# W2's weight tiles requested one by one, six tiles ahead of TensorE

## The chip, the core and the metric

The kernel runs on one core of one Trainium2 chip. The metric is the device time of one execution in microseconds; where several executions are shown, their median is given. All operands are bf16 in HBM and all sums are f32 in PSUM.

## The reference

The program computes `x + A(LN(x)) + B(LN(x))` for a sequence of 2048 rows of width D = 576. A is a causal attention with 32 heads of 18 columns and a sliding window of 256 positions. B is a gated feed-forward block with F = 4608 hidden columns. The part that matters here is B's last product, whose weight is W2.

```python
xn = _layernorm(x)                                  # 2048 x 576
# A: sliding-window attention, 32 heads of 18 columns, window 256
o  = softmax(mask(q @ k.T * 18**-0.5)) @ v          # q, k, v = xn @ wqkv
A  = o @ wo                                         # wo: 576 x 576
# B: gated feed-forward
h  = silu(xn @ w1) * (xn @ w3)                      # 2048 x 4608
B  = h @ w2                                         # w2: 4608 x 576
out = x + A + B
```

## The kernel before, in words

The sequence is cut into NC = 4 blocks of 512 rows, and each block c goes through two phases (for every block but the first, a projection to q, k and v stands ahead of them).

**Phase 1** makes the hidden tiles. For u = 0 to 35, TensorE multiplies one 128-column slice of w1 and w3 with the normalised rows (`unit_pairs`, line 670), ScalarE takes a tanh (line 679), and VectorE forms a tile of `hT` (lines 685 and 688). Attention scores, exponentials, masks and three of four P·V groups are worked in between.

**Phase 2** sums the block's output. `p2_list` writes its order out by hand: two halves of 288 output columns, and in each half nine W2 tiles and then the four `wo` steps of the attention output. A W2 tile is 512 rows by 288 columns (288 KB, loaded by one DMA in `load_w2`, line 347). TensorE spends 32 matmuls on it (line 736: four 128-row slices, four row tiles of the output, each in two halves of 64 rows). So a block uses 18 W2 tiles, numbered 0 to 17. After a tile's 32 matmuls the list has an item `next`, at which the program asks for a later tile. The items that carry matmuls are counted by `n`, which starts at -3 and is raised by one behind each of them: two items of `wo` come first, then 16 for each W2 tile. After `n == 19` the last P·V group is put in (line 611), and its result is turned, scaled and sent to `oT` by the SP queue (line 658). Behind `n == 40` the SP queue sends a transposed piece of the next block's rows (line 392), from `n == 170` on it loads six parts of the next block's w1 and w3 (line 315), and at `n == 300` it swaps halves of the rows (line 399). Outputs are added by VectorE (line 755) and written by the SP queue (line 757).

**Buffers and order.** Eight slots hold W2 tiles: four of their own (`w2`) and four (`w2x`) laid over the second w1/w3 buffer, which is free once phase 1 has ended. `w2_at` gives tile i the slot i modulo 8. The tiles 0 to 3 are asked for during the block before (for block 0, in phase 1 on the SP queue). The tiles 4 to 17 are asked for in phase 2 on ScalarE's DMA queue, which works in program order:

- tiles 4 and 5 at the start of phase 2, behind the last matmul of phase 1 (an explicit wait, `after=(last_pe(),)`);
- tile `sl + 6` at the `next` item of tile `sl`, for `sl` = 0 to 11. No wait is written there; the only wait comes from the slot, which must have been read: tile i waits for the last matmul of tile i - 8. The tiles 6 and 7 have no such predecessor in their block.
- at the items of tiles 13, 14, 16 and 17, the next block's tiles 0 to 3, which wait for the slots of this block's tiles 10, 11, 16 and 17.

`_Prog.add` collects the dependencies of each operation, and `resolve` turns them into semaphore waits: an operation waits for the last one of each engine that it depends on, and each engine executes in program order. `last_pe()` is the operation that was added last for TensorE.

```python
                if sl + AHEAD < 2 * NFC:
                    load_w2(c, sl + AHEAD)
                elif sl in (13, 14, 16, 17):
                    load_w2(c + 1, sl - 13 if sl < 16 else sl - 14)
```

Of the kernel before, what the change touches and what calls it, by code (L numbers as in the profile page):

```python
# [44 lines left out]
class _Prog:  # L45
# [13 lines left out]
    def add(self, eng, fn, r=(), w=(), j=(), dma=None, after=()):  # L59
        deps = []  # L60
        for k in r:
            deps += self.bufs[k].writers
        for k in w:
            g = self.bufs.get(k)
            if g is not None:
                deps += g.ahead(eng)
        for k in j:
            g = self.bufs[k].before
            if g is not None:
                deps += g.ahead(eng)  # L70
        op = _Op(eng, fn, deps + list(after), dma)
        op.after = tuple(after)
        self.n[eng] += 1
        op.pos = self.n[eng]
        if dma is not None:
            self.dma_count[dma] = self.dma_count.get(dma, 0) + 16
            op.cnt = self.dma_count[dma]
        for k in r:
            self.bufs[k].readers.append(op)
        for k in w:  # L80
            self.bufs[k] = _Gen([op], self.bufs.get(k))
        for k in j:
            self.bufs[k].writers.append(op)
        for k in w:
            if self.bufs[k].before is not None:
                self.bufs[k].before.before = None
        self.ops.append(op)
        return op
# [76 lines left out]
def bass_parallel_sum__sliding_block__glu_gated_swiglu__prompt_kernel(  # L165
# [32 lines left out]
    with ExitStack() as es:  # L198
# [4 lines left out]
        NXP, NOF, NPT, NW13, NW2, NOD, AHEAD = 7, 4, 10, 3, 4, 2, 6  # L203
# [120 lines left out]
        def last_pe():  # L324
            return next(o for o in reversed(P.ops) if o.eng == "pe")
# [9 lines left out]
        def w2_at(c, i):  # L335
            n = i % (2 * NW2)
            if n < NW2:
                s = (n + 2 * c) % NW2
                return s, w2[s]
            return n, w2x[:, n - NW2, :, :]  # L340

        def load_w2(c, i, eng="act", after=()):
            if c >= NC:
                return
            s, dst = w2_at(c, i)
            half, fc = divmod(i, NFC)
            add(eng, lambda e: e.dma_start(
                dst[:, :, :], B_w2[fc * 512:(fc + 1) * 512, half * HD:(half + 1) * HD].rearrange("(fl p) d -> p fl d", p=128)),
                w=[("w2", s)], after=after, dma=f"w2_{s}")
# [183 lines left out]
        def keep_keys(g):  # L533
            add("pool", lambda e: e.tensor_copy(
                kb4[:, g, :, :].bitcast(dt.float32), kv[:, g, 2 * NB - NV:NB, :].bitcast(dt.float32)),
                r=[("k", g)], w=[("kp", g)])
# [82 lines left out]
        def pv_out(b, i):  # L619
            add("dve", lambda e: e.transpose(uqs[i], PS[:, b, :]), r=[("ps", b)], w=uq_keys[i])  # L620

        def o_scale(i):
            u3 = uqs[i].rearrange("p (n d) -> p n d", d=32)
            o3 = oq[:, :].rearrange("p (n d) -> p n d", d=32)[:, :, 0:Dh]
            add("dve", lambda e: e.reciprocal(rden[:], u3[:, :, Dh]), r=uq_keys[i], w=["rden"])  # L625
            add("pool", lambda e: e.tensor_tensor(  # L626
                o3, u3[:, :, 0:Dh], rden[:].unsqueeze(2).to_broadcast([128, CH // 32, Dh]), ALU.mult),
                r=uq_keys[i] + ["rden", "oq0"], w=["oq"])

        def o_turn(g, half):  # L630
            i = g // 2 % NOD
            c0 = half * (CH // 2)
            add("dve", lambda e: e.transpose(od[i][:, g % 2, c0:c0 + CH // 2], oq[:, c0:c0 + CH // 2]),  # L633
                r=["oq", "oq0"], **{"j" if half or g % 2 else "w": [("od", i)]})
# [21 lines left out]
        def o_pack(j, eng, n0=0, n1=4):  # L656
            for n, (dst, src) in list(enumerate(pack_moves(j)))[n0:n1]:
                add(eng, lambda e, dst=dst, src=src: e.dma_start(dst, src),
                    r=[("od", j % NOD), "oTz"], dma=f"oT{j}", **{"j" if n else "w": [("oT", j)]})
# [72 lines left out]
        def p2_mm(bank, half, r, stat, move, keys):  # L732
            new = (bank, half) not in summed
            held = [op for x, op in summed.get((bank, half), {}).items() if x != r]
            tile = {} if r is None else {"tile_position": (64 * r, 0)}
            op = add("pe", lambda e: e.matmul(PS[:, bank, 0:HD], stat, move, start=new, stop=False, skip_group_check=True, **tile),  # L736
                     r=keys, after=held if r is not None else (), **{"w" if new else "j": [("ps", bank)]})
            summed[(bank, half)] = {r: op}

        def p2_item(c, item, xs):  # L740
            nonlocal of_ctr
            what, half, k, n, turn, fc = item
            d0 = half * HD
            if what == "next":
                sl = half * NFC + fc
                if sl + AHEAD < 2 * NFC:
                    load_w2(c, sl + AHEAD)
                elif sl in (13, 14, 16, 17):
                    load_w2(c + 1, sl - 13 if sl < 16 else sl - 14)
            elif what == "out":  # L750
                o = of_ctr % NOF
                of_ctr += 1
                t = c * TB + n
                bank = ACC[half][n]
                add("dve", lambda e: e.tensor_tensor(ofin[:, o, :], PS[:, bank, 0:HD], xp[xs[n]][:, d0:d0 + HD], ALU.add),  # L755
                    r=[("ps", bank), ("xp", xs[n])], w=[("of", o)])
                add("sp", lambda e: e.dma_start(out2[t * 128:(t + 1) * 128, d0:d0 + HD], ofin[:, o, :]),
                    r=[("of", o)], dma=f"out{o}")
            else:
                for r in range(2) if turn is not None else (None,):  # L760
                    tt = n if r is None else 2 * n + (r ^ turn)
                    rows = slice(0, 128) if r is None else slice(64 * r, 64 * r + 64)
                    cols = slice(tt * 128, (tt + 1) * 128)
                    if what == "w2":
                        f = fc * 4 + k
                        buf, wt = w2_at(c, half * NFC + fc)
                        args = hT[rows, f, cols], wt[rows, k, :], [("h", f), ("w2", buf)]
                    elif what == "wo":
                        js = range(3 if half == 0 and k < 2 else G // 2)
                        args = oT[rows, k, cols], wo[rows, k, d0:d0 + HD], [("oT", j) for j in js] + ["oTz", "wo"]  # L770
                    else:
                        args = oT[rows, 4, cols], wo[rows, 4, d0:d0 + HD], [("oT", 0), "oTz", "wo"]
                    p2_mm(ACC[half][tt], half, r, *args)
# [110 lines left out]
        for c in range(NC):  # L884
# [145 lines left out]
            if c + 1 < NC:  # L1030
                for g in range(G):
                    keep_keys(g)
            for i in range(NW2, AHEAD):
                load_w2(c, i, after=(last_pe(),))
            banks = ()
            n = -3
            for item in p2_list(c):
                p2_item(c, item, xs)
                if item[0] == "next":
                    continue  # L1040
                n += 1
                if n == 3:
                    for u in sorted(side):
                        for what in side.pop(u):
                            what()
                elif n == 19:
                    banks = jobs[NF - 2]
                    pv(c, 3, banks)
                    pv_out(banks[0], 0)
                    pv_out(banks[1], 1)  # L1050
                    o_scale(0)
                    o_turn(6, 0)
                    o_turn(6, 1)
                    o_scale(1)
                    o_turn(7, 0)
                    o_turn(7, 1)
                    o_pack(3, "sp")
                elif n == 40 and c + 1 < NC:
                    xn_send((c + 1) * TB + 3)
                elif n == 300 and c + 1 < NC:  # L1060
                    xn_swap(c + 1, ("sp", "sp"))
                elif n in (100, 120) and c + 2 < NC:
                    t = (c + 2) * TB + (n == 120)
                    xslot[t] = load_x(t)
                elif n in (170, 195, 220, 245, 270, 295) and c + 1 < NC:
                    load_part((last_pe(),))
# [31 lines left out]
```

## Time and profile before

| what | value |
|---|---|
| time, median of 3 runs | 561.2 us (560.73 to 562.16) |
| the profiled execution: its own time | 559.42 us |
| the profiled execution: span, first to last instruction | 557.7 us |
| TensorE's matmuls busy | 552.4 us, 99% of the span |
| mean granted TensorE clock | 0.999 |
| W2 tiles on ScalarE's DMA queue | 68, of 288 KB each |

The span is the time from the first to the last instruction; the profiled execution's own time is 1.7 us longer. An engine's busy time is the union of its instructions. A DMA issue is shown on the queue of the engine that issues it (ACTq, SPq), with the time from issue to landing; neighbouring issues of one line are merged into one row of the timeline. A wait is put down to the engine and the line that ended it. Idle time of an engine that is not the bound costs nothing by itself.

### The profile page before, as it was taken

The numbers are of one execution on the slowest core, as the hardware profiler recorded it, in microseconds if no ns is written. First come the engines' busy times: TensorE is split into PE (matmuls) and PEld (weight loads), VectorE is DVE, ScalarE is ACT, GpSimd is POOL, SyncE is SP. The second block draws the span as 40 slices with busy tenths as digits, with TensorE's granted clock in tenths as the row PEclk, the third lists the DMA queues.
The fourth block names the chain that finished last, engine by engine and source line by source line (L and its number), as shares of the span: only waits on it lengthen the run. The fifth ranks groups of instructions, "written<-read, shape, count | busy, mean of one in ns | idle before, by whom it ended". The sixth has DMA issues, their size and how long they took to land.

```text
span 557.7 us, 18215 instructions
## 1 busy us (share of the span) xinstructions
PE 552.4 (99%) x8015; PEld 350.5 (63%) x8015; DVE 310.8 (56%) x584; ACT 253.1 (45%) x349; POOL 163.1 (29%) x383
## 2 busy tenths in 40 slices
PE   8999999999999999999999999999999999999998
PEld 4445455677687555489876645547777654555776
DVE  7466788710365778851046668884105567767211
ACT  4357776100287776600037777650005667675000
POOL 6313454400033445330003344533000333433000
PEclk9999999999999999999999999999999999999999
DMA  9998899866566455667656746467764674551740
GB/s 249 208 191 182 191 197 225 177 182 150 140 141 146 130 149 152 151 186 191 149 112 138 171 109 169 126 162 196 182 152 82 136 170 123 152 135 33 204 108 22
DMA packets 127893, 86.07 MB, mean 154 GB/s; under 512 B 35430, under 2 KB 125502, under 8 KB 127814
## 3 DMA queue, kind: packets, MB, share of 16 engines
q1 hardware_dynamic: 89890, 63.17, 48.7%
q10 hardware_dynamic: 37924, 21.73, 15.2%
q8 instruction: 63, 1.03, 0.8%
q14 instruction: 16, 0.13, 0.1%
HBM read 71.37 MB, written 2.36 MB: 132 GB/s over the span
## 4 chain that ended last, share of the span: by engine, by line
PE 98%; DVE 1%; DMA 0%; POOL 0%; issue 0%
PE ps L670 50%; PE ps L736 29%; PE ps L434 9%; PE ps L554 6%; PE ps L611 4%; DMA xp<-in_A_x_dram 0%; DVE xn L367 0%; DVE stats L355 0%; DVE stats L357 0%; DVE mv L358 0%; POOL rstd L361 0%; PE ps L379 0%; DVE ofin L755 0%; POOL vpe L359 0%; DVE vpe L359 0%
## 5 line engine op out<-in xcount | busy, mean ns | idle before, releaser
L670 PE MATMUL ps<-xnT,w 64*128 64x512 bf16 x1400 | 182.0, 376 | 0.0
L670 PE MATMUL ps<-xnS,w 64*128 64x512 bf16 x1120 | 155.0, 376 | 0.0
L736 PE MATMUL ps<-w,hT 64*128 64x288 bf16 x2288 | 143.8, 283 | 0.0
L685 DVE SCALAR_TENSOR_TENSOR gs<-th,ps 128x512 bf16<-128x512 bf16 x144 | 98.0, 680 | 80.4 <-ACT th L679 79.5
L563 ACT ACTIVATE pt<-ps 128x1024 bf16<-128x1024 f32 (+1 forms) x112 | 113.1, 1010 | 63.4 <-PE ps L554 63.0
L736 PEld LDWEIGHTS ps<-w,hT 64*128 64x128 bf16 x2288 | 116.1, 94 | 25.2 <-issue 0.2
L670 PEld LDWEIGHTS ps<-xnT,w 64*128 64x128 bf16 x1400 | 72.8, 94 | 56.0
L590 POOL TENSOR_TENSOR pt<-pt,mk 128x128 int32<-128x128 int32 (+1 forms) x199 | 80.4, 426 | 79.4 <-ACT pt L563 79.4
L688 DVE SCALAR_TENSOR_TENSOR hT<-gs,ps 128x512 bf16<-128x512 bf16 x144 | 98.9, 687 | 4.9
L679 ACT ACTIVATE th<-ps 128x512 bf16<-128x512 f32 x144 | 85.4, 593 | 23.9 <-PE ps L670 23.7
L670 PEld LDWEIGHTS ps<-xnS,w 64*128 64x128 bf16 x1120 | 59.3, 94 | 50.9
L755 DVE TENSOR_TENSOR ofin<-ps,xp 128x288 bf16<-128x288 f32 x32 | 12.7, 451 | 121.3 <-PE ps L736 121.3
L447 ACT ACTIVATE stage<-ps 128x512 bf16<-128x512 f32 x16 | 9.6, 597 | 143.6 <-PE ps L434 143.6
L590 POOL TENSOR_TENSOR hT<-hT,mk 128x128 int32<-128x128 int32 (+1 forms) x31 | 12.4, 420 | 167.8 <-ACT hT L563 167.8
L554 PE MATMUL ps<-qv,kv 64*128 64x320 bf16 (+4 forms) x528 | 53.6, 260 | 0.0
L554 PEld LDWEIGHTS ps<-qv,kv 64*128 64x128 bf16 x528 | 28.1, 94 | 24.9 <-ACT pt L563 0.5
L434 PE MATMUL ps<-xnT,wp 64*128 64x512 bf16 (+1 forms) x360 | 39.0, 355 | 0.0
L563 ACT ACTIVATE stage<-ps 128x1024 bf16<-128x1024 f32 x24 | 24.6, 1023 | 12.6 <-PE ps L554 12.6
L633 DVE STREAM_TRANSPOSE od<-oq 128x256 bf16<-128x256 bf16 x64 | 25.8, 427 | 6.3 <-POOL oq L626 6.3
L434 PEld LDWEIGHTS ps<-xnT,wp 64*128 64x128 bf16 x360 | 20.3, 94 | 12.8
L626 POOL TENSOR_TENSOR oq<-uq,rden 128x288 bf16<-128x288 f32 x16 | 10.8, 672 | 38.7 <-DVE rden L625 38.7
L590 POOL TENSOR_TENSOR stage<-stage,mk 128x128 int32<-128x128 int32 (+1 forms) x42 | 17.0, 422 | 17.3 <-ACT stage L563 17.2
(58 smaller groups left out, 346.6 us busy)
## 6 DMA issues: line engine op xcount, KB each, us to landing
w<-in_B_w_dram SPq DMA_DIRECT2D x210, 192.0 KB, 3.9
w<-in_B_w_dram ACTq DMA_DIRECT2D x68, 288.0 KB, 3.6
xp<-in_A_x_dram SPq DMA_DIRECT2D x29, 144.0 KB, 3.2
out_dram<-ofin SPq DMA_DIRECT2D x32, 72.0 KB, 2.8
xnS<-xnT SPq DMA_DIRECT2D x8, 256.0 KB, 5.2
oT<-od SPq DMA_DIRECT2D x56, 36.0 KB
pt<-in_A_wqkv_dram SPq DMA_DIRECT2D x4, 288.0 KB, 6.5
hT<-in_B_w_dram SPq DMA_DIRECT2D x6, 192.0 KB, 7.9
```

The source lines that it names most:

```text
L434: op = add("pe", lambda e, out_=out_, st=st, mv=mv, n=n, r0=r0, first=first: e.matmul(out_, st, mv, start=first, stop=(part == 1 and n == ...
L554: add("pe", lambda e, r0=r0, out_=out_, kb=kb, q0=q0, nb=nb: e.matmul(out_, kb4[r0:r0 + 64, g, kb + NV - NB, :] if kb < 0 else kv[r0:r0 + ...
L563: add("act", lambda e: e.activation(pt_slot(sl)[:, 0:w, :], PS[:, SC[0]:SC[1] + 1, 0:w].rearrange("p r q -> p q r"), ACT.Exp, scale=scale) ...
L590: add("pool", lambda e, vb=vb, mm=mm: e.tensor_tensor(vb, vb, mm, ALU.mult), r=(key if n == 0 else []) + ["mk"], **{"w" if n == 0 else "j" ...
L611: add("pe", lambda e, p=p, q=q, pr=pr, sl=sl, g=g, pos=pos, q0=q0, nb=nb, col=col, first=first, n=n: e.matmul(PS[32 * q:32 * q + VW, banks ...
L633: add("dve", lambda e: e.transpose(od[i][:, g % 2, c0:c0 + CH // 2], oq[:, c0:c0 + CH // 2]), r=["oq", "oq0"], **{"j" if half or g % 2 els ...
L670: op = add("pe", lambda e, n=n, r0=r0, r=r, k=k, src=src: e.matmul(PS[:, b0 + r, :], wt[r0:r0 + 64, k, fl * 128:(fl + 1) * 128], src, star ...
L679: add("act", lambda e: e.activation(th[i][:], PS[:, bg, :], ACT.Tanh, scale=0.5), r=[("ps", bg)], w=[("th", i)])
L685: add("dve", lambda e: e.scalar_tensor_tensor(out=gs[i][:], in0=th[i][:], scalar=1.0, in1=PS[:, bg, :], op0=ALU.add, op1=ALU.mult), r=[("t ...
L688: add("dve", lambda e: e.scalar_tensor_tensor(out=hT[:, u, :], in0=gs[i][:], scalar=0.5, in1=PS[:, bu, :], op0=ALU.mult, op1=ALU.mult), r= ...
L736: op = add("pe", lambda e: e.matmul(PS[:, bank, 0:HD], stat, move, start=new, stop=False, skip_group_check=True, **tile), r=keys, after=he ...
L755: add("dve", lambda e: e.tensor_tensor(ofin[:, o, :], PS[:, bank, 0:HD], xp[xs[n]][:, d0:d0 + HD], ALU.add), r=[("ps", bank), ("xp", xs[n] ...
```

## The change

Every request of phase 2 now waits for TensorE. At the `next` item of tile `sl`, the request for tile `sl + 6` waits for the operation that was added last for TensorE, which there is the last matmul of tile `sl`. At the start of phase 2 only tile 4 is asked for; tile 5 is asked for behind `n == 9`, that is after ten of tile 0's sixteen items. The slots, the order of the requests on their queue, the number of bytes and everything on the other engines stay as they were.

```diff
             if what == "next":
                 sl = half * NFC + fc
                 if sl + AHEAD < 2 * NFC:
-                    load_w2(c, sl + AHEAD)
+                    load_w2(c, sl + AHEAD, after=(last_pe(),))
                 elif sl in (13, 14, 16, 17):
                     load_w2(c + 1, sl - 13 if sl < 16 else sl - 14)
...
-            for i in range(NW2, AHEAD):
-                load_w2(c, i, after=(last_pe(),))
+            load_w2(c, NW2, after=(last_pe(),))
             banks = ()
             n = -3
             for item in p2_list(c):
...
+                elif n == 9:
+                    load_w2(c, AHEAD - 1, after=(last_pe(),))
                 elif n == 19:
```

## The prediction

> **What bounds the kernel now.** I read the page's sums and slices first, then the chain that ended last, then the waits of TensorE alone.
>
> ```profile
> span 557.7 us, 18215 instructions
> PE 552.4 (99%) x8015; PEld 350.5 (63%) x8015; DVE 310.8 (56%) x584; ACT 253.1 (45%) x349; POOL 163.1 (29%) x383
> ...
> PE   8999999999999999999999999999999999999998
> ...
> ACT  4357776100287776600037777650005667675000
> ...
> PEclk9999999999999999999999999999999999999999
> DMA  9998899866566455667656746467764674551740
> ...
> PE 98%; DVE 1%; DMA 0%; POOL 0%; issue 0%
> ```
>
> The reader is to see that TensorE has work in every slice, at full clock, and that the chain that ended last is TensorE's to 98%. Nothing that is off TensorE can shorten the time, unless TensorE waits for it. The zeros in ScalarE's row are the four second phases: ScalarE computes nothing there, so its queue is free to stand in a wait.
>
> A busy row may hide stalls, so the waits of TensorE come next. These two are all that the view of waits lists for its matmuls in the whole span.
>
> ```profile
> PE ps L379 <- DVE xn L367: 1.3, 2, 0.9
> PE ps L790 <- DVE oq L785: 1.2, 1, 1.2
> ```
>
> Both lines belong to the opening (line 790 warms the array up, line 379 transposes the first rows). No W2 tile was ever waited for. The matmuls' timeline in the first block's second phase says the same:
>
> ```profile
> 101.78 0.41 PE L736 MATMUL ps<-wo,oT 64*128 64x288 bf16 x4
> 102.03 2.61 PE L736 MATMUL ps<-w,hT 64*128 64x288 bf16 x40
> 104.57 1.05 PE L611 MATMUL ps<-pt,va 64*20 64x320 bf16 x72
> 105.55 15.37 PE L736 MATMUL ps<-w,hT 64*128 64x288 bf16 x248
> 120.75 2.12 PE L736 MATMUL ps<-wo,oT 64*128 64x288 bf16 x32
> 122.71 17.80 PE L736 MATMUL ps<-w,hT 64*128 64x288 bf16 x288
> 140.35 2.37 PE L736 MATMUL ps<-wo,oT 64*128 64x288 bf16 x36
> 142.56 3.19 PE L434 MATMUL ps<-xnT,wp 64*128 64x512 bf16 x28
> ```
>
> The rows follow each other without a hole, and the next block's projection (line 434) follows at once. In the chain, the long pieces of the four second phases are:
>
> ```profile
> 105.62 37.10 PE ps L736 x604
> ...
> 242.98 37.13 PE ps L736 x604
> ...
> 380.24 37.10 PE ps L736 x604
> ...
> 517.54 37.47 PE ps L736 x572
> ```
>
> One matmul takes 37.10 / 604 = 0.0614 us, and a W2 tile of 32 matmuls 1.96 us. That is the clock by which the change asks for tiles.
>
> **The change part by part.** It moves requests; no byte, buffer or matmul is added or taken away. The old request times are the rows of ScalarE's queue. The first two rows below are its second to fifth issue of this phase (tiles 5 to 8) with their landing times; the next two are the timeline behind them; the last is the landing time of all 72 W2 tiles.
>
> ```profile
> L347 ACTq DMA_DIRECT2D w<-in_B_w_dram x4: 522/530/1343, 102.4 to 104.9; - x4
> ...
> DMA to landing us min/median/max: 4.1/4.6/5.0
> ...
> 104.94 0.52 ACTq L347 DMA_DIRECT2D w<-in_B_w_dram  x1
> ...
> 107.24 2.33 ACTq L347 DMA_DIRECT2D w<-in_B_w_dram  x2
> ...
> DMA to landing us min/median/max: 2.9/3.7/6.2
> ```
>
> So tiles 5 to 7 are asked for in a pile from 102.4, behind tile 4 at the start of the phase; tile 8 follows at 104.94 (its slot was free when tile 0 ended, but it had to come behind the pile), tile 9 at 107.24 when tile 1 ended, and so on.
>
> *Tile 4* is asked for as before, behind phase 1's last matmul. Cost 0.
>
> *Tile 5* moves from about 102.4 to the end of tile 0's twentieth matmul: 102.03 + 20 × 0.0614 = 103.26, and some 0.2 us until ScalarE's queue has seen it, so 103.5. It is used when tiles 0 to 4 are done. From the timeline: 40 matmuls are tile 0 and 8 of tile 1; the other 24 of tile 1 run from 105.55 to 107.02; tile 5 starts at 107.02 + 3 × 1.96 = 112.9. That leaves 9.4 us for a transfer that took at most 6.2 us anywhere. Cost 0, covered by the matmuls of tiles 1 to 4.
>
> *Tiles 6 and 7* move from the pile to the ends of tiles 0 and 1, about 104.2 and 107.2. Tile 6 starts at 107.02 + 4 × 1.96 = 114.9, so its window is 10.7 us (the P·V group lies in it). Tile 7 starts at 116.8; its window is 9.6 us.
>
> *Tiles 8 to 17* waited for the end of tile i - 8 and now wait for tile i - 6. Each is asked for two tiles, 3.9 us, later. From request to use lie five whole tiles, 5 × 1.96 = 9.8 us, less the 0.2 us of the queue: 9.6 us. For tiles 9 to 14 the `wo` steps lie in between too (122.71 - 120.75 = 2.0 us). The tightest windows are thus 9.4 and 9.6 us, 3.2 us over the longest landing of the trace and 5.7 us over its median. Cost 0; the cover is TensorE's own work on the five tiles between.
>
> *What is queued behind the new waits.* ScalarE's queue has nothing but W2 requests until the next block's projection, as its zeros show. The next block's tiles 0 and 1, which went out when tiles 10 and 11 ended, now stand behind tile 17 and go out with it when tile 11 ends: three requests at once, the first of them 2.0 us later than it was. They are used a whole block later. Tiles 2 and 3 of the next block still wait for tiles 16 and 17, so the queue is done as early as before, and the projection's copies on ScalarE are not held up.
>
> *What else shares the transfers.* SP's queue runs beside it.
>
> ```profile
> 110.41 2.97 SPq L658 DMA_DIRECT2D oT<-od  x4
> 113.42 1.21 SPq L392 DMA_TRANSPOSE xnT<-xn  x1
> ...
> 125.83 13.84 SPq L315 DMA_DIRECT2D w<-in_B_w_dram  x6
> 139.78 1.18 SPq L399 DMA_DIRECT2D xnS<-xnT  x2
> ...
> 161.76 1.84 PE ps L670 x16
> ```
>
> Three requests at 128.8 now fall among the six of line 315, where there was one. Those six fill a w1/w3 buffer of the next block, whose phase 1 starts at 161.76 in the chain below, 20 us behind the last of them at 139.8. The oT pieces of 110.4 are used in the `wo` steps at 120.75 and meet the same one tile per 1.96 us as before. I take 0 for all of them.
>
> *New signals.* TensorE must raise a semaphore behind `n == 9` in each block and, in the last block, behind tiles 10 and 11: six more signals. No row shows their price. The nearest row is the spread of the matmuls that raise some and those that raise none:
>
> ```profile
> L736 PE MATMUL ps<-w,hT x2288: 279/283/297, 102.0 to 554.1; 64*128 64x288 bf16 x190, 128*128 128x288 bf16 x1
> ```
>
> At most 297 - 283 = 14 ns each, 0.08 us in all; at least nothing. I take 0; even the upper end is far below what can be measured.
>
> *Can it gain?* The pile at 102.4 goes. What it could have cost TensorE is read from windows of 2 us with a different load of transfers (columns: matmuls busy and their count, weight loads, clock, DMA share, GB/s; line 736 alone):
>
> ```profile
> 106.00:108.00 2.00, 2.00 (x36) 1.59 (x34) 1.00 1.15 301
> 108.00:110.00 2.00, 2.00 (x38) 1.59 (x34) 1.00 1.17 305
> ...
> 136.00:138.00 2.00, 2.00 (x36) 1.60 (x34) 1.00 0.21 53
> ```
>
> Under 305 GB/s TensorE does as many matmuls in 2 us as under 53 GB/s (the count includes those cut by the edges). So the pile costs it nothing, and there is nothing to give back. As a bound: if every matmul of line 736 fell from the median 283 to the shortest 279 ns, 1.4% of that line's 143.8 us would go, 2.0 us.
>
> ```profile
> L736 PE MATMUL ps<-w,hT 64*128 64x288 bf16 x2288 | 143.8, 283 | 0.0
> ```
>
> *A rule against the change.* The row says that a tile landed 2.9 to 6.2 us after its request, with 9.4 us or more to spare for it. The Trainium skill, page "DMA: Bandwidth & Descriptors", section "Rules for kernel authors", advises to issue a transfer early and wait for it late, so that its fixed cost overlaps with compute; the change issues later. By the rule the change can only lose, by the row it loses nothing until a landing outlasts its window. The sum stays 0 by both as long as the landings keep to the rows, and the first rival is the case where they don't.
>
> **The sum.** 0 for every part: the profiled execution stays at 559.42 us (span 557.7 and 1.7 around it). The median of the runs shown is 561.2, 1.8 above that execution, and the forecast is set against the median: **561.2 us**, no change. About 0.3% (1.7 us) is what a measurement of this kernel can tell from no change; the three runs span 1.4 us.
>
> **The rivals.**
>
> *A late tile (slower).* With six tiles outstanding instead of up to eight, a landing time L over 9.6 us stops TensorE. Tile 7 or 8 would then be L - 9.6 late; the tiles behind it are shifted with it and lose nothing more, until tile 15, asked for on the shifted end of tile 9, is late again. That is twice in a block and 8 × (L - 9.6) over four blocks. It passes 0.3% from L = 9.8 on. Twice the longest landing, 12.4 us, would give 8 × 2.8 = 22 us, about 584 us. For it speaks that landings grow when requests meet: 4.1 to 5.0 in the pile against 2.9 at the least. Against it: the longest median of any load in the list of issues is 7.9 us, at the opening where the DMA row has nines, and the change makes the requests of phase 2 meet less, but for three at the end of tile 11.
>
> ```profile
> w<-in_B_w_dram ACTq DMA_DIRECT2D x68, 288.0 KB, 3.6
> ...
> hT<-in_B_w_dram SPq DMA_DIRECT2D x6, 192.0 KB, 7.9
> ```
>
> Chance 0.11. This is the mechanism by which the rule of the Trainium skill just named would decide against the change; so far the trace has no landing near the window.
>
> *Less crowding (faster).* Transfers that write SBUF or compete for HBM could slow TensorE in a way the 2 us windows are too coarse for. The bound is the 2.0 us above, 559.2 us. Against it: the same counts under 305 and 53 GB/s. Chance 0.07.
>
> *The waits don't move the requests.* If the issues were set by something other than TensorE, for instance by the queue's own pace (0.5 us for one in the pile), the new waits would already be met. The old issues from 107.24 on, one in 2 us, speak against it: they follow the tiles. The time would be 561.2 too. Chance 0.04.
>
> **How the numbers follow.** All hidden, as forecast: 0.78. With the third rival that is 0.82 within 0.3%; slower 0.11 from the late tile; faster 0.07 from less crowding. Within the likeliest case the median of a few runs moves as the three runs do, from 560.7 to 562.2. The range that leaves out no more than 2 in 10 reaches halfway to the faster rival's 559.2 and as far the other way, for a late tile of a fraction of a microsecond: 559.8 to 562.8.
>
> **What would show it.** After the change ScalarE's queue should have one issue at 102.0, one at about 103.5, one at about 104.2, then 107.2 and on by 1.96 us, and three together at 128.8. The landings of tiles 6 to 8 should fall from 4.1–5.0 towards 3 us. TensorE's long pieces of line 736 should stay at 37.1 us. A wait of line 736 for a W2 transfer would prove the first rival; a piece shorter than 37.0 us the second; a changed time with unchanged second phases would mean that something outside the change's reach moved, and that the prediction has no name for it.

## The result, and the profile after

| | before | changed |
|---|---|---|
| median of 13 runs each | 560.81 us | 559.62 us |
| lowest to highest | 559.56 to 563.42 | 559.43 to 560.24 |
| profiled execution, its own time | 559.42 us | 559.62 us |
| span of that execution | 557.7 us | 557.9 us |

The ratio is 0.9978, with a 95% interval of 0.9968 to 0.9988: faster by 0.2%, 1.2 us. The shortest executions of the two kernels lie 0.13 us apart; what the change took away are the longer ones. The profiled execution of before was shorter than every one of its 13 timed runs, and the profile of the changed kernel, which is an ordinary execution of it, looks like it. The page of the changed kernel:

```profile
span 557.9 us, 18215 instructions
PE 553.4 (99%) x8015; PEld 350.3 (63%) x8015; DVE 310.9 (56%) x584; ACT 253.1 (45%) x349; POOL 163.5 (29%) x383
...
PEclk9999999999999999999999999999999999999999
DMA  9998899768566457657856746565684674641650
```

The waits of its matmuls, all that are listed, and the long pieces of its four second phases in the chain (start, length, line, matmuls):

```profile
PE ps L790 <- DVE oq L785: 1.2, 1, 1.2
PE ps L379 <- DVE xn L367: 0.4, 1, 0.4
```

```profile
105.67 37.10 PE ps L736 x604
...
243.09 37.29 PE ps L736 x604
...
380.50 37.10 PE ps L736 x604
...
517.72 37.47 PE ps L736 x572
```

No W2 tile is waited for. Only the second block (block 1, since blocks are numbered from 0) differs, 37.29 against 37.13 us, and it is longer. ScalarE's queue shows that the requests moved as the change says; the timeline of that queue, in narrow windows, and the landing times of the second and third issue, of the three together at 128.85, and of all 72:

```profile
102.05 0.40 ACTq L347 DMA_DIRECT2D w<-in_B_w_dram  x1
...
103.51 0.38 ACTq L347 DMA_DIRECT2D w<-in_B_w_dram  x1
...
104.25 0.38 ACTq L347 DMA_DIRECT2D w<-in_B_w_dram  x1
...
107.29 0.37 ACTq L347 DMA_DIRECT2D w<-in_B_w_dram  x1
...
128.85 1.49 ACTq L347 DMA_DIRECT2D w<-in_B_w_dram  x3
...
DMA to landing us min/median/max: 3.4/3.5/3.6
...
DMA to landing us min/median/max: 4.7/6.1/7.3
...
DMA to landing us min/median/max: 2.9/3.6/7.7
```

So the schedule is the one that was worked out, and it explains nothing by itself: in these two executions TensorE loses nothing to W2, before or after. The gain lies in executions that the two profiles don't show, and the experiments had to find what lengthens those.

### The profile page after: what moved, and what is told of

Its sections match the earlier page's. It is cut to its first block, busy times and chain, and to the rows that moved or that the text cites. A ratio compares the mean times of both kernels' runs of the same rounds, so it can differ in the third digit from the quotient of the medians.

```text
span 557.9 us, 18215 instructions
## 1 busy us (share of the span) xinstructions
PE 553.4 (99%) x8015; PEld 350.3 (63%) x8015; DVE 310.9 (56%) x584; ACT 253.1 (45%) x349; POOL 163.5 (29%) x383
## 3 DMA queue, kind: packets, MB, share of 16 engines
q8 instruction: 63, 1.03, 0.8%
## 4 chain that ended last, share of the span: by engine, by line
PE 98%; DVE 1%; DMA 0%; POOL 0%; issue 0%
PE ps L670 50%; PE ps L736 29%; PE ps L434 9%; PE ps L554 6%; PE ps L611 4%; DMA xp<-in_A_x_dram 0%; DVE xn L367 0%; DVE stats L355 0%; DVE stats L357 0%; DVE mv L358 0%; POOL rstd L361 0%; PE ps L379 0%; DVE ofin L755 0%; POOL vpe L359 0%; DVE vpe L359 0%
```

## The experiments

Twelve kernels were timed, each beside the kernel before on the same chip. "Ratio" is to the kernel before.

| run | median (lowest to highest), us | before beside it | ratio, 95% interval |
|---|---|---|---|
| e1 before, again | 560.56 (559.49 to 565.80) | 560.46 | 1.0001 (0.9976 to 1.0026) |
| e2 pile gone, then eight ahead | 559.69 (559.50 to 561.28) | 560.46 | 0.9978 (0.9957 to 0.9999) |
| e3 pile kept, then six ahead | 561.06 (559.78 to 563.29) | 560.46 | 0.9992 (0.9969 to 1.0016) |
| e4 pile kept, P·V group later | 559.55 (559.38 to 560.20) | 560.62 | 0.9977 (0.9968 to 0.9986) |
| e5 changed, other pile at the start | 560.45 (559.83 to 560.93) | 560.62 | 0.9995 (0.9986 to 1.0004) |
| e6 changed, other pile mid-phase | 560.04 (559.88 to 560.64) | 560.62 | 0.9989 (0.9980 to 0.9998) |
| e7 before, pile doubled | 560.79 (559.97 to 566.14) | 560.62 | 1.0009 (0.9990 to 1.0029) |
| e8 changed, and P·V group later | 559.55 (559.38 to 560.04) | 560.13 | 0.9985 (0.9974 to 0.9996) |
| e9 e8, other pile at the group | 559.96 (559.70 to 560.17) | 560.13 | 0.9991 (0.9982 to 1.0000) |
| e10 e8, other pile mid-phase | 560.03 (559.85 to 561.09) | 560.13 | 0.9998 (0.9989 to 1.0006) |
| e12 pile whole, behind the group | 559.54 (559.36 to 562.92) | 560.60 | 0.9980 (0.9962 to 0.9999) |
| e13 changed, only tile 4 ahead of the group | 559.55 (559.44 to 559.97) | 560.60 | 0.9979 (0.9967 to 0.9990) |

### Which half of the change: e1, e2, e3

e1 is the kernel before, unchanged. e2 takes the changed kernel's waits for the tiles 6 and 7 (and its place for tile 5), and leaves the later ones out:

```diff
-                    load_w2(c, sl + AHEAD, after=(last_pe(),))
+                    load_w2(c, sl + AHEAD, after=(last_pe(),) if sl < 2 else ())
```

e3 takes the kernel before, with the pile at the start, and adds the waits from tile 8 on:

```diff
-                    load_w2(c, sl + AHEAD)
+                    load_w2(c, sl + AHEAD, after=(last_pe(),) if sl >= 2 else ())
```

> The kernel before, unchanged. The profiled execution of before (559.42 us) is as short as that of the changed kernel (559.62 us), while the medians of 13 runs differ by 1.2 us (560.81 and 559.62) and the runs of before reach from 559.56 to 563.42. Theory A (a delay that strikes only some executions of before, from the pile of four W2 requests at the start of the second phase): this kernel scatters again, median 560.4 to 561.2 us, spans between 557.7 and 561. Theory B (the difference belongs to the occasion, not to the kernel): median within 0.3 us of the changed kernel's 559.6.

> The pile at the start of the phase taken away, and nothing else of the lag: tile 5 behind n == 9, tiles 6 and 7 behind tiles 0 and 1, and from tile 8 on no added wait (so tiles 8 and 9 go out together with tile 7 when tile 1 ends, and tiles 10 to 17 eight ahead as before). Theory A (the pile at the phase's start costs): the whole gain, 559.6 us, with little scatter. Theory C (it is the lag of six, which takes load off the later part of the phase): no gain, 560.4 to 561.2 us. Theory B: all within 0.3 us.

> The opposite half: tiles 4 to 7 asked for at once at the start of the phase, as before, and tiles 8 to 17 six ahead, as in the changed kernel. Theory A: no gain, 560.4 to 561.2 us with the scatter of before. Theory C: the whole gain, 559.6 us. Theory B: all within 0.3 us.

The kernel before scatters again (559.49 to 565.80), so the difference belongs to the kernel. e2 has the whole gain. e3 has none at the median: the interval of its own ratio would still allow 0.3%, but its median is 1.4 us above that of e2 (95% interval 0.2 to 1.7). Theory A holds. It is the pile of four requests at the start of the phase; the lag of six behind it is worth nothing that was measured.

The traces now gave a first sight of the loss. The timeline of e1's weight loads in the second block, behind the P·V group, and the row of the queue that carries instructions in the window 242.65 to 242.75 (packets, MB, share of 16 engines in the window):

```profile
243.34 1.71 PEld L736 LDWEIGHTS ps<-w,hT 64*128 64x128 bf16 x30
245.46 0.83 PEld L736 LDWEIGHTS ps<-w,hT 64*128 64x128 bf16 x14 [0.42 <-issue]
...
q8 instruction: 1, 0.02, 83.2%
```

TensorE stands still for some 0.3 us before 245.46, and nothing that the profile shows released it ("issue"). A packet of the instruction queue began at 242.7 and took 83.2% of 16 × 0.1 us, 1.33 us, so it ended at 244.03; the hole ends 1.43 us later. That queue as a whole, in the kernel before:

```profile
q8 instruction: 63, 1.03, 0.8%
```

63 packets and 1.03 MB, for 8015 matmuls and 8015 weight loads, are 64 bytes for each of these 16030 instructions; so I take it to be TensorE's program, fetched in pieces of 256 instructions while it runs. The spacing agrees: in every trace 31.8 × 256 matmuls and weight loads are started between the starts of the 25th and the 57th packet, that is in 32 packets. In every trace that has a hole in the second block it stands behind the same instruction, 26.60 × 256 matmuls and weight loads into the program.

That gives an estimate of how far ahead TensorE fetches. In the traces of e2, e6, e12 and e13, where the packet is not late, it starts when 25.61 to 25.71 × 256 instructions have been started, and the holes stand at 26.60, one packet later. At the rate of W2's matmuls 256 instructions last 128 × 0.0614 = 7.9 us. But the P·V group begins at 25.62, and 192 of these 256 instructions are its own, so here they are used up in about 3.2 us: the holes of block 1 begin 3.15 us behind the group's start.

### Is it the instructions: e4, e5, e6, e7

e4 moves the P·V group (and the rest of its branch) in the kernel before:

```diff
-                elif n == 19:
+                elif n == 56:
                     banks = jobs[NF - 2]
```

e5, e6 and e7 add four transfers of 216 KB that nobody reads, in the blocks 1 to 3, into attention buffers that are dead there. In e5 they stand behind the changed kernel's request for tile 4, in e6 behind `n == 99`, in e7 behind the kernel before's requests for tiles 4 and 5:

```diff
+            def load_more(after=()):
+                for m in range(4 if c else 0):
+                    add("act", lambda e, m=m, sl=free[m - 4]: e.dma_start(
+                        pt_slot(sl).rearrange("p q r -> p (q r)")[:, 0:3 * HD].rearrange("p (k d) -> p k d", d=HD),
+                        B_w2[m * 384:(m + 1) * 384, 0:HD].rearrange("(fl p) d -> p fl d", p=128)),
+                        w=pt_keys(free[m - 4]), after=after, dma=f"more{m}")
...
             load_w2(c, NW2, after=(last_pe(),))
+            load_more()
...
+                elif n == 99:
+                    load_more((last_pe(),))
```

> The kernel before with its pile of W2 requests kept, and one thing moved: the last P.V group (and what follows it) stands behind n == 56 instead of n == 19, so some 4.6 us later, when W2 tiles are asked for one by one. In the traces so far the only holes in TensorE's second phases lie 3.2 us behind the start of that group, with the releaser 'issue', and they end 1.37 to 1.43 us after the end of a 16 KB packet of the queue that carries instructions (q8). Theory D (the pile delays a fetch of TensorE's instructions, and the P.V group, short matmuls at 15 ns each, uses instructions up faster than anything else in the phase): the scatter goes, 559.4 to 559.8 us. Theory E (the pile delays something else, a W2 tile or a buffer): the pile is as it was, so 560.4 to 561.2 us with scatter.

> The changed kernel, with four further transfers of 216 KB (rows of W2) put at the start of the second phase in blocks 1 to 3, behind the request for tile 4, into attention buffers that are dead there; nobody reads them. It is a pile of about the old size that carries nothing TensorE needs. Theory D: slow again, 560.4 to 562 us with scatter, and holes of line 736 with the releaser 'issue' about 3.2 us behind the P.V group. Theory E: 559.6 us, as the changed kernel.

> The same four further transfers, asked for at once behind n == 99 (some 7 us after the P.V group), where TensorE only works on W2 tiles. Theory D: TensorE uses instructions up slowly there, so a late fetch has time; 559.5 to 559.9 us, as the changed kernel. If a pile costs wherever it stands (plain load on the transfers, or on SBUF): as much as the pile at the start.

> The kernel before, with the same four transfers put behind the requests for tiles 4 and 5 at the start of the phase in blocks 1 to 3: the pile doubled. Theory D: the fetch is later still in nearly every execution; 562 us or more, with holes behind the P.V group in two or three of the three blocks of the trace, of 0.3 us or more each. If the pile only makes W2 tiles late: holes at the starts of tiles 5 to 8 with a transfer as the releaser. If neither: 560.5 us.

e4 keeps the pile and has the whole gain, 559.55 us with a scatter of 0.8 us. So the pile costs nothing once the P·V group stands later. Why isn't shown by e4 alone, because it also moves the group against the packets: in the second block the instruction at 26.60 then starts 5.5 us after the one a packet earlier, against 3.4 us with the group at its old place. In e5 transfers that TensorE doesn't need bring the holes back. A late W2 tile is ruled out by where the holes stand: 5 to 14 matmuls into tile 2, in e1, e3, e5 and e7, and that tile was asked for a block earlier.

The medians of e5, e6 and e7 carry an artefact of the added transfers. In block 3 a copy of the projection overwrites one of the buffers that they filled, and ScalarE has one more semaphore to wait for ahead of it. The copy starts some 0.4 us later than in the changed kernel, though the transfers landed long before. From the end of the third block's second phase to the start of the fourth's it takes 96.62, 96.61 and 96.63 us, against 96.25 in the changed kernel. One row of the waits in e6, in the window 417 to 430, is that wait:

```profile
PEld ps L434 <- ACT stage L447: 0.4, 1, 0.4
```

Without these 0.36 us e6, which missed its range (559.5 to 559.9), would stand at 559.7, level with the changed kernel, and e5 at 560.1, under its range but 0.5 above the changed kernel. e5 lies 0.41 us over e6, as expected in sign, though by the runs alone the difference is not certain (95% interval -0.1 to 0.9); its trace has the holes and e6's has none.

e7 missed in size: 560.79, not 562, and some 0.3 us of it are the artefact. A pile 1.75 times as large (2016 KB against 1152) didn't make the median measurably worse than the pile alone, and of the holes in its trace one is above 0.3 us. Its trace has the plainest hole. The timeline of matmuls around the group in the second block, and the instruction queue in the window 242.85 to 242.95:

```profile
241.85 0.32 PE L611 MATMUL ps<-stage,va 64*20 64x320 bf16 x4
...
242.24 0.98 PE L611 MATMUL ps<-pt,va 64*20 64x192 bf16 x68
243.16 2.01 PE L736 MATMUL ps<-w,hT 64*128 64x288 bf16 x29
245.89 0.54 PE L736 MATMUL ps<-w,hT 64*128 64x288 bf16 x6 [0.73 <-issue]
...
q8 instruction: 1, 0.02, 101.8%
```

The group's 96 matmuls go by in 243.16 - 241.85 = 1.31 us, 13.6 ns each, where W2's take 61.4. So they use up instructions four to five times as fast. The packet began at 242.9, took 1.018 × 1.6 = 1.63 us and ended at 244.53; TensorE went on at 245.89, 1.36 us later. The waits of e7 and of e2, which has no pile at the start, for comparison:

```profile
PEld ps L736 <- issue: 1.5, 3, 1.0
PE ps L736 <- issue: 0.7, 1, 0.7
```

```profile
PEld ps L736 <- issue: 0.4, 2, 0.2
```

### Moving the place: e8, e9, e10

e8 is the changed kernel with the group behind `n == 56`. e9 and e10 add the four transfers to e8, behind `n == 55` and behind `n == 99`.

```diff
-                elif n == 19:
+                elif n == 56:
...
+                elif n == 55:
+                    load_more((last_pe(),))
```

> The changed kernel with the last P.V group behind n == 56 as well. Theory D (late fetches of TensorE's instructions behind the P.V group): both remedies against the same delay, so hardly more than either, 559.4 to 559.6 us; and the hole of 0.07 us that the changed kernel still had in its second block is gone. If the two act on different things: 558.6 us or less.

> The kernel of both remedies, with four further transfers of 216 KB asked for behind n == 55, just ahead of the moved P.V group, in blocks 1 to 3. The further transfers alone cost 0.36 us in block 3's projection, which waits for them (96.61 against 96.25 us from phase 2 to phase 2 in the traces so far). Theory D: in the traces so far all holes of block 1 stand behind the same instruction of TensorE, 26.60 times 256 matmuls and weight loads into the program. With the group moved, the next such place, 27.60, comes some 7 us behind the group's start and its fetch falls into the pile, so a hole can appear there, at 253 us, where none has been; 560.0 to 560.8 us. If the hole belonged to the instruction at 26.60 itself: no hole, 559.8 to 560.0 us.

> The same with the four further transfers behind n == 99, away from the P.V group. Theory D: no hole; 559.8 to 560.0 us, that is the kernel of both remedies and the 0.36 us of the projection's wait. If a pile costs wherever it stands: as much as the kernel with the pile at the group.

e8 shows no hole and no second gain, 559.55 us: both remedies act on the same delay. e9 didn't show the hole that theory D allowed: 559.96 us, e8 plus about the 0.36 us of the artefact, and no hole, which is the outcome named for a hole that belongs to the instruction at 26.60 itself. That rival falls by other traces: e3 and e5 have a hole in block 3, both at 58.45 × 256, and e7 one in block 2, at 42.53. In e9 the packet in question began at 248.9 us in the second block, as in e8 without the added transfers. It ended 3.8 us behind the group's start, and the instruction one packet on (27.60) was started 6.3 us behind it, so there was time to spare. e10 has nearly the same median, 560.03, and in its trace a wait of another kind. The P·V group stands late in this kernel, so the pieces of `oT` go out at 527.46 us, the pile follows from 528.12, and TensorE waits for a piece once:

```profile
PE ps L736 <- DMA oT<-od: 0.7, 1, 0.7
```

### The pile on the other side of the group: e12, e13

e12 is the kernel before with all of its pile, asked for behind `n == 20`, right behind the P·V group. e13 is the changed kernel with tiles 5 and 6 asked for there.

```diff
                 sl = half * NFC + fc
+                if sl == 0:
+                    return
...
-            for i in range(NW2, AHEAD):
-                load_w2(c, i, after=(last_pe(),))
...
+                elif n == 20:
+                    for i in range(NW2, AHEAD + 1):
+                        load_w2(c, i, after=(last_pe(),))
```

In e13 the loop runs over `(AHEAD - 1, AHEAD)` and tile 4 stays at the start.

> The kernel before with its pile kept whole and shifted: tiles 4 to 7 asked for together, but behind n == 20, one item after the last P.V group, some 4 us later than before. In the traces so far the instruction packet next to that group starts 0.0 to 0.2 us behind the group's start where no pile stands ahead of it and 0.5 to 1.3 us where one does; holes came only where it ended more than 1.75 us behind the group's start in block 1, and each ended 1.3 to 1.5 us after the packet's end. Theory D: the packet is issued before the pile, so it starts within 0.2 us and there are no holes; 559.4 to 559.8 us with little scatter. If a pile of W2 requests costs by itself: 560.1 us or more. Tile 4 then has little time to spare (about 1 us by the landings so far), and a wait of line 736 for a transfer would be that and not the pile.

> The changed kernel with tiles 5 and 6 asked for behind n == 20 as well, so that only tile 4 is asked for ahead of the P.V group. Theory D: the changed kernel's last small hole (0.07 us, its packet started 0.65 us behind the group's start) goes: 559.4 to 559.6 us, about 0.1 us under the changed kernel.

e12 has the whole gain at the median with the whole pile, and the group at its old place: what counts is the order of the pile and the group with its fetch. The chain's long pieces of its four phases, the instruction queue in the window 241.35 to 241.45, and the landing times of all its W2 tiles:

```profile
105.75 37.10 PE ps L736 x604
...
243.09 37.10 PE ps L736 x604
...
380.32 37.10 PE ps L736 x604
...
517.55 37.47 PE ps L736 x572
...
q8 instruction: 1, 0.02, 58.4%
...
DMA to landing us min/median/max: 3.0/5.5/7.8
```

The packet started at 241.4, 0.3 us ahead of the group (which starts at 241.7 in this trace), and took 0.584 × 1.6 = 0.93 us. The W2 tiles land later than in any other kernel, 5.5 us in the median, and no tile is waited for.

e13's trace has no hole, and its median, 559.55, can't be told from the changed kernel's. That tiles 5 and 6 made the changed kernel's hole of 0.07 us isn't shown by it: e2 and e6 ask for them at the same places as the changed kernel and have no hole either.

The same two readings for all traces with the group at its old place; "start" is the start of the packet next to the group behind the group's own start, and a hole is the time between two matmuls' starts beyond 0.12 us:

| trace | start of the packet in blocks 1, 2, 3, us | holes in blocks 1, 2, 3, us |
|---|---|---|
| before | 0.50, 0.72, 1.04 | 0, 0, 0 |
| e1 before, again | 0.67, 0.61, 0.83 | 0.28, 0, 0 |
| e3 pile kept | 0.82, 0.93, 1.21 | 0.19, 0, 0.16 |
| e7 pile doubled | 1.02, 0.82, 0.82 | 0.89, 0.09, 0 |
| e5 other pile at the start | 1.02, 0.67, 1.30 | 0.32, 0, 0.22 |
| changed kernel | 0.65, 0.02, 0.37 | 0.07, 0, 0 |
| e2 pile gone | 0.06, 0.17, 0.01 | 0, 0, 0 |
| e6 other pile mid-phase | 0.04, 0.00, 0.01 | 0, 0, 0 |
| e12 pile behind the group | -0.31, 0.05, -0.02 | 0, 0, 0 |
| e13 only tile 4 ahead | 0.09, 0.03, 0.06 | 0, 0, 0 |

With a pile ahead of the group the packet starts 0.5 to 1.3 us late. With the tiles asked for one by one or behind the group it starts within 0.2 us, except for 0.65 and 0.37 us in the changed kernel. All eight holes end 1.29 to 1.51 us after their packet's end. A late packet doesn't always make one: in block 2 of e3 it ended 2.24 us behind the group's start without a hole, where e7's ended at 1.98 and made 0.09 us. In the profiled execution of before the packets were late too, and in block 1 its packet ended 1.75 us behind the group's start, where the changed kernel's, at 1.82, already made a hole: the execution that the prediction read stood at the brink and happened to lose nothing.

**What stays open.** The size of the gain isn't accounted for by traces. Where there are holes they sum to 0.1 to 1.0 us per execution. The one ordinary execution of before that was traced, e1's (560.44 us), has a span 0.7 us longer than the changed kernel's, and of that 0.2 us are the hole and 0.4 us a later opening. The longest runs of before, up to 565.8 us, were never the profiled ones, and that their excess is made of the same holes is argued from e2, e4 and e12, which keep their medians at 559.5 to 559.7. Even there single runs of e2 and e12 reached 561.3 and 562.9, and why is not known. Nor is it known why the changed kernel's packets in blocks 1 and 3 came later than those of e2 and e6, which ask for the same tiles ahead of the group. The start of the first second phase also moved between 101.73 and 102.24 us from trace to trace, in kernels of both kinds; that scatter belongs to the opening. Where the 1.4 us from the packet's end to the next matmul go, no trace shows.

None of e4, e8, e12 and e13 (559.54 to 559.55) can be told from the changed kernel (559.62): with the holes gone, the rest is TensorE's own 552 to 553 us of matmuls and the opening.

## Why the prediction was wrong

- **The forecast of no change was wrong**, narrowly: the time fell to 559.62 us where the range ended at 559.8, and the interval of the ratio excludes 1. The fall of 0.2% is smaller than the 0.3% that was said to be indistinguishable; thirteen runs of each kernel could tell more than that.
- **The step that failed** is "So the pile costs it nothing, and there is nothing to give back". It looked for a cost in the rate of W2's matmuls and found none, rightly: 36 and 38 matmuls in 2 us under 301 and 305 GB/s, and 36 under 53. The cost was of another kind. The pile delays a fetch of instructions while the P·V group uses up, at 13.6 ns a matmul, those that TensorE still has, and TensorE stops for 0.1 to 0.9 us, 3.1 to 3.7 us behind that group's start. The prediction had the row of the group (72 matmuls in 1.05 us) and never asked what feeds it, and it didn't list the instruction queue among those beside which the pile runs.
- **The setting of the sum** was the second fault. The profiled execution was 1.8 us under the median of the runs shown, and the text said so and went on to argue from that execution that nothing was lost. An execution shorter than the others is evidence that the others lose something which it does not show; the 1.2 us gained are most of the 1.4 us by which it lies under the median of 13 runs. The other 0.4 us is that the median of the three runs lay above that of the 13.
- **Less crowding**, the rival on the faster side, had the right sign and a bound (559.2 us) that the result respects, with the wrong mechanism, so its sign was right by luck: the windows show no slower matmuls, and what the holes follow is a late fetch.
- **The late tile** didn't come, as argued. The windows of 9.4 and 9.6 us held against landings of up to 7.7 us, and e12 shows that even tiles asked for 4 us after the phase's start are in time. The three requests at once at 128.85 landed in 4.7 to 7.3 us, the longest of them beyond the 6.2 that was the most before; nothing waited for them.
- **The waits do move the requests**: the issues at 103.5, 104.2, 107.3 and 128.8 came where they were put, and the tiles 5 and 6 landed in 3.4 to 3.6 us.
- "A piece shorter than 37.0 us the second" was a bad test. No trace has a shorter one than 37.1 us, e2 and e12 included, and the loss was in pieces that are longer, which the profile of before didn't hold. So the time changed beside second phases that look unchanged, and nothing outside the change's reach has to have moved for that.
- The cost of the signals was put at nothing, and no run speaks against it; none measures it alone.

## What to carry to other kernels

Before saying that a pile of transfers costs nothing because nobody waits for its data, look at the queue that carries the instructions: a busy engine's program is a transfer too, and a burst of short instructions behind a pile is where it can come too late. Put large requests behind such a burst, or spread them, or move the burst away; here each of the three gave the same 0.2%. And when the profiled execution is shorter than the median of the runs, read the scatter as part of the question, since the profile can't contain what the other executions lost.

## What the runs showed of the hardware that was not expected

- TensorE's instructions come in 63 packets of 16 KB on a queue of their own, as worked out above, one for 256 matmuls and weight loads, which is 7.9 us of W2's matmuls. Behind a pile of requests of 1152 to 2016 KB a packet started 0.5 to 1.3 us late, and where TensorE had stopped it went on 1.3 to 1.5 us after the packet's end. The Trainium skill, page "DMA: Bandwidth & Descriptors", section "Issuing engines are not separate DMA queues", says that transfers issued by different engines run on the same 16 DMA engines and interleave; the late packets agree, on a queue on which the program itself issues nothing.
- Doubling the pile (e7, 560.79 us) cost no more at the median than the pile (560.62 beside it): by the packet starts, 0.8 to 1.0 us late against 0.5 to 1.0 in before, it seems to count that transfers are queued when the fetch is asked for, and little how many follow.
